# A segment-recurrent attention and gMLP kernel: a PSUM bank for the last V piece, another order of the V matmuls, and a new home for three side jobs

## The chip, the cores and the metric

The kernel runs on one core of one Trainium2 chip. The metric is the device time of a run in microseconds (us). Before the change nine runs have a median of 910.12 us, from 907.9 to 913.51.

Engine names in the profile: PE is TensorE (matrix multiply), PEld its weight load, ACT is ScalarE, DVE is VectorE, POOL is GpSimd, SP is SyncE, from whose queue (SPq) the transfers are issued.

## The reference

Two blocks run after each other on 2048 tokens of width 512. The first is attention with a recurrent memory: tokens come in 64 segments of 32, and the 8 memory rows that a segment uses are the first 8 output rows of the segment before. The second is a gated mixer over all tokens.

```python
for s in range(64):                        # recurrent: mem comes from the step before
    h = concat([mem, ln(x)[32*s:32*s+32]])  # 8 + 32 rows, 512 wide
    q, k, v = h @ Wq, h @ Wk, h @ Wv        # 32 heads of 128
    p = softmax(where(mask, q @ k.T * scale, -1e9))
    o = (p @ v) @ Wo
    mem = o[:8]; outs.append(o[8:])
h = x + concat(outs)
z = gelu(ln(h) @ w_in)
z1, z2 = z[:, :896], ln(z[:, 896:])
h2 = h + (z1 * (w_sp @ z2 + b_sp)) @ w_out
```

## The kernel before, in words

One function, `fast_path`, writes the program as a list of operations for each engine, in the order in which the Python code calls them. A helper class, `Emitter`, gives each operation the waits that its reads and writes need. A PSUM bank is one token `("ps", b)`: who writes a bank waits for all earlier readers of that bank. Each engine works through its list in order, so the order written by hand in the segment loop is the schedule.

The work has three stages: weights and first projections (to about 70 us of the trace), the segment loop (64 segments, to about 720 us), the mixer (the rest). The change lies in the segment loop.

Not all of a segment's 32 new rows need the chain of segments. In each segment only a 32-row piece of 8 memory rows and the first 24 x rows (`hT`) goes through the projections in the loop. The last 8 x rows of every segment are projected ahead, for 16 segments at a time: "X projections", in Q and K form (`qkx_mm`, L405, into `QTx`) and in V form (`vx_mm`, L424, through the DRAM buffer `vext_d` into `Vx`). The first 32 segments' X work is done before the loop; the rest is cut into 48 groups, in the list `gx`: 16 V groups for segments 0 to 15, then 32 Q/K groups for segments 16 to 47. Each loop step takes one group, in four PE parts and one eviction.

One segment `s` (with `j4 = s % 4`, `rb = s // 4`) runs as follows.

1. `QK` (L472): five pieces of Q and K matmuls, in 32-column tiles that run four at a time. After the first 8 matmuls stands `mem_out(s-1, 1)` (L648), which brings the second half of the new memory into `hT` (ACT, L656; the first half is copied by DVE, L654). Then come the operations that the previous segment left in the list `late`.
2. `QK_evac`: ACT copies each piece to `Tst` (L483), DVE transposes it to `QT` or `KT` (L491).
3. `S_half(s, 0)`: scores of heads 0 to 15 into bank 5 (L519, L525). ACT takes the exponent (`sm_exp`, L532). PE computes V of these heads (`V_half(s, 0)`, 16 matmuls of 512 columns, L573, bank 6), then the row sums (`sm_sums`, L539, L544). ACT takes the logarithm (`sm_ln`, L551) and the exponent of its negative (`sm_rcp`, L555); `sm_norm` multiplies on DVE (L559) and POOL (L563).
4. The same for heads 16 to 31, with V in two pieces: `V_half(s, 1)` into bank 2, evicted by DVE (L584), and into bank 7, evicted by ACT (L582). The second row sums stand in the middle of that last piece.
5. Two parts of the X group, then `PV_half(s, 0)` and `PV_half(s, 1)` (L592, L598; row tiles, four banks 0, 1, 6, 7, one per 32-row strip), then two more parts of the X group.
6. `cT_evac` (ACT L612, DVE L614): six evictions. `Wo` (L627): 56 and 8 matmuls, with `part_evac` (ACT, L639) and `mem_out(s, 0)` between.
7. Every fourth segment: `F_group` and `WoX_scatter` (L662, L687) gather the outputs of the previous four segments in bank 4, `F_add` (L667, DVE) adds x. `WoX_mm` (L677) is the Wo product of the X rows of four segments, a quarter (8 matmuls of 512 columns) at the end of each segment. `h_done` (L691 to L697) takes the statistics of the finished rows and stores them; `xn2_apply` and `xn2_store` (L700, L705) normalise and store them for the mixer.
8. x for two row blocks ahead: `load_x` at `j4 == 0`; at the end of `j4 == 1` `ln_inplace` (DVE statistics L353, L354, POOL power L355, L357, DVE apply L363); at the end of `j4 == 2` four PE transposes `xT` (L373), and in `late` an ACT copy from PSUM into `hT` (`ring_copy`, L383).

SP's queue in the loop: the load of `Vx` for two segments ahead (L446), x loads, stores of h and xn2, and one piece of the mixer's weight per odd segment (`wT_piece`, a transposing transfer L721 and a store L722). After segment 48 it also carries transposing transfers of xn2 (L714).

Of the kernel before, what the change touches and what calls it, by code (L numbers as in the profile page):

```python
# [169 lines left out]
def fast_path(nc, st, keep, A_x, A_mem0, A_Wq, A_Wk, A_Wv, A_Wo, A_seg_len, B_w_in, B_w_sp, B_b_sp, B_w_out, out):  # L170
    S = A_x.shape[1]
    D = A_x.shape[2]
# [80 lines left out]
    vext_d = nc.dram_tensor("vext_d", [NCK, 128, H * DH], BF, kind="Internal").ap()  # L253
    xn2_d = nc.dram_tensor("xn2_d", [RB, 128, D], BF, kind="Internal").ap()
    h_d = nc.dram_tensor("h_d", [RB, 128, D], BF, kind="Internal").ap()
    wT_d = nc.dram_tensor("wT_d", [S // 64, 128, RB, 64], BF, kind="Internal").ap()

    ps = st.enter_context(nc.psum_tensor("f_ps", [128, 8, 512], F32))
# [5 lines left out]
    def PB(b):  # L264
        return ("ps", b)
# [111 lines left out]
    def slot(s):  # L377
        return s % NSLOT

    def ring_copy(rb, bank):  # L380
        src = psb[:, bank, 0:512].rearrange("p (dc s c) -> p s dc c", dc=DC, s=4, c=SEG)[:, :, :, 0:XM]
        s0 = slot(4 * rb)
        act(lambda e: e.activation(out=hT[:, s0:s0 + 4, :, M:32], in_=src, func=ACT.Copy),  # L383
            reads=[PB(bank)], writes=[("hTx", rb % 3)])
# [14 lines left out]
    def qkx_mm(ck, i, bank, hhs=range(4)):  # L399
        mi, h0 = i // 8, 4 * (i % 8)  # L400
        ws = (w_q, w_k)[mi]
        for hh in hhs:
            h = h0 + hh
            for dc in range(DC):
                pe(lambda e, h=h, dc=dc, hh=hh: e.matmul(ps[:, bank, hh * 128:(hh + 1) * 128], lhsT=ws[:, dc, h * DH:(h + 1) * DH],  # L405
                                                         rhs=hTe[:, ck % 3, dc, :], start=(dc == 0), stop=(dc == DC - 1)),
                   reads=[("hTe", ck % 3), ("W", mi, h // 8)], writes=[PB(bank)])
# [44 lines left out]
    SB = 5  # L452
    UBK = (0, 1)
    PVB = (0, 1, 6, 7)
    VB = {(0, 0): 6, (1, 0): 2, (1, 1): 7}
    OB = 2
    XB = 3
    WXB = 4
# [95 lines left out]
    def sm_rcp(b):  # L554
        act(lambda e: e.activation(out=R_sb[:, b, :], in_=R_sb[:, b, :], func=ACT.Exp, scale=-1.0, bias=RBIAS),  # L555
            reads=[("R", b)], writes=[("R", b)])
# [113 lines left out]
    def load_h(rb):  # L670
        sp(lambda e: e.dma_start(hbuf[:, rb % 2, :], xr[:, rb, :]), writes=[("h", rb % 2)])

    def WoX_mm(rb, qr):
        for bg in range(8):
            b, g = bg // 4, bg % 4
            h = 16 * b + 4 * qr + g
            pe(lambda e, h=h, g=g, i=8 * qr + bg: e.matmul(ps[32 * g:32 * g + 32, WXB, :], lhsT=cTx[:, rb % 2, i, :], rhs=w_o[:, h, :],  # L677
                                                           start=(i < 4), stop=(i >= H - 4), tile_position=(0, 32 * g)),
               reads=[("cTx", rb % 2), ("Wo", h // 8)], writes=[PB(WXB)])
# [111 lines left out]
    gx = []  # L791

    def qkx_group(ck, i):
        gx.append([lambda hh=hh: qkx_mm(ck, i, XB, (hh,)) for hh in range(4)] + [lambda: qkx_evac(ck, i, XB, "dve")])

    def vx_group(ck, n):
        gx.append([lambda dc=dc: vx_mm(ck, n, XB, dc) for dc in range(DC)] + [lambda: vx_evac(ck, n, XB, "dve")])
# [21 lines left out]
               writes=[("wT", tb % 2, t)], after=after)  # L819

    lastop = {}
    qx_copy(0)
    for s in range(NSEG):
        j4 = s % 4
        rb = s // 4
        if j4 == 1 and rb > 0:
            load_h(rb - 1)
        if s == NSEG - 1:
            load_h(rb)
        if s % 2 == 1 and s // 2 < NWT:  # L830
            wT_piece(s // 2)
        if j4 == 0 and 2 <= rb + 2 < RB:
            load_x(rb + 2, 0)
        if s == 1:
            load_xe(3, 1)

        QK(s, QKP[0], (0, 1))
        if s > 0:
            mem_out(s - 1, 1)
            for f in late:  # L840
                f()
        QK(s, QKP[1], (0, 1))
        QK(s, QKP[0], (2, 3))
        QK_evac(QKP[0])
        QK(s, QKP[1], (2, 3))
        QK_evac(QKP[1])
        for piece in QKP[2:]:
            QK(s, piece)
            lastop["qk"[piece[3]]] = em.by_eng["pe"][-1]
            QK_evac(piece)  # L850
        if s == NSEG - 1:
            load_wT(0, [lastop["q"]])
        if s == 0:
            mask_pe()
        S_half(s, 0)
        sm_exp(0)
        V_half(s, 0)
        V_evac(0, "dve")
        sm_sums(0)
        sm_ln(0)  # L860
        S_half(s, 1)
        lastop["s"] = em.by_eng["pe"][-1]
        sm_exp(1)
        sm_rcp(0)
        if s == NSEG - 1:
            sp(lambda e: e.dma_start(w_in1, winr[:, :, 0:FH]), writes=["w_in1"], after=[lastop["s"], lastop["x"]])
            sp(lambda e: e.dma_start(bsp_b, bass.AP(B_b_sp.tensor, B_b_sp.offset, [[0, 128], [1, S]])), writes=["bsp"], after=[lastop["k"]])
            for r in range(8, RB - 2):
                xn2T_dma(r, [lastop["s"], lastop["x"]])
        V_half(s, 1, gs=(0, 2))  # L870
        V_evac(1, "dve", (0, 2))
        V_half(s, 1, (0, 1), gs=(2, 4))
        sm_sums(1)
        sm_ln(1)
        sm_rcp(1)
        V_half(s, 1, (2, 3), gs=(2, 4))
        lastop["v"] = em.by_eng["pe"][-1]
        V_evac(1, "act", (2, 4))
        sm_norm(0)
        sm_norm(1)  # L880
        if s + 1 < NSEG:
            qx_copy(s + 1)
            lastop["x"] = em.by_eng["pool"][-1]
# [29 lines left out]
        if j4 == 3 and rb > 0:  # L913
            late.append(lambda rb=rb: h_done(rb - 1))
        late += xs[4:]
        if j4 == 1 and 2 <= rb + 2 < RB:
            ln_inplace(0)
        if s == 3:
            ln_inplace(1)
# [3 lines left out]
        if s == 5:  # L923
            xT(1, FBK)
            late.append(lambda: xe_copy(3, FBK))
        if s + 1 < NSEG and s >= 3:
            WoX_mm((s + 1) // 4 - 1, (j4 + 1) % 4)
            if j4 == 2:
                late.append(lambda rb=rb: WoX_evac(rb - 1))
        if s + 1 == NSEG:  # L930
            for f in late:
                f()
        if s + 2 < NSEG:
            load_vx(s + 2)
        if j4 == 0 and rb >= 2:
            xn2_apply(rb - 2, rb % 2)
            xn2_store(rb - 2, rb % 2)
# [932 lines left out]
```

## Time and profile before

| | us |
|---|---|
| median of nine runs | 910.12 |
| the profiled execution, its own time | 914.51 |
| its span, first to last instruction | 912.8 |
| from the first to the last copy L654 (62 segments) | 649.0 |
| PE busy | 863.7 |
| PEld busy | 536.5 |
| DVE busy | 508.9 |
| ACT busy | 453.0 |
| POOL busy | 152.9 |

All lines of the profile come from one execution. A line of a timeline has the start in us, the busy time, the engine, the line of the code, the operation, out<-in with shapes, a count, and in brackets the engine's idle time before it with what ended it. A line of a table of stretches has start:end, length, then for PE, PEld, DVE, ACT and POOL the busy time with the number of instructions, then the granted PE clock, the share of the transfer engines, and GB/s. Matmuls overlap in the array, so the starts of PE's instructions tell more than their busy times.

### The profile page before, as it was taken

Reading aid. Unit: us, or ns where it says so; the run is one execution under the profiler, and the core shown is the slowest. Engines: PE = TensorE matmul, PEld = TensorE weight load, DVE = VectorE, ACT = ScalarE, POOL = GpSimd, SP = SyncE. Lnnn points to the kernel's source line nnn. Section 1 sums busy time; section 2 is a strip of 40 time slices with the busy share of each in tenths; the row PEclk is TensorE's granted clock in tenths of the full one; section 3 lists DMA queues with packets and bytes.
Section 4 is the critical chain, followed back from the end, with each engine's and each line's share of the span. In section 5 each row is a group of like instructions: output and inputs, shape, how many; then the busy total and the mean of one; then the engine's idle time right before and its main releaser. Section 6 shows DMA issues by size and latency. Waiting matters only on the chain.

```text
span 912.8 us, 48903 instructions
## 1 busy us (share of the span) xinstructions
PE 863.7 (95%) x22506; PEld 536.5 (59%) x22513; DVE 508.9 (56%) x1231; ACT 453.0 (50%) x1274; POOL 152.9 (17%) x403
## 2 busy tenths in 40 slices
PE   6989999999999999999999999889988999999998
PEld 6665566566666666666666666555555544444443
DVE  2435656565666666566656666555556554453433
ACT  2335566655565655666555656565666665400000
POOL 1401111121211211111212111121112122200000
PEclk9999999999999999999999999999999999999999
DMA  9971221322213020312112230514021392021201
GB/s 327 381 197 44 55 56 45 70 59 60 65 33 68 22 70 19 77 36 53 50 44 51 41 68 22 107 39 93 19 70 50 116 280 65 1 98 59 75 12 37
DMA packets 99587, 71.50 MB, mean 78 GB/s; under 512 B 62249, under 2 KB 84913, under 8 KB 99377
## 3 DMA queue, kind: packets, MB, share of 16 engines
q1 hardware_dynamic: 99376, 68.32, 27.5%
q8 instruction: 178, 2.92, 1.4%
q14 instruction: 33, 0.26, 0.1%
HBM read 39.46 MB, written 18.61 MB: 64 GB/s over the span
## 4 chain that ended last, share of the span: by engine, by line
PE 84%; ACT 8%; DVE 5%; issue 2%; POOL 1%; DMA 0%; SPq 0%; ACTq 0%
PE f_ps L472 21%; PE f_ps L627 14%; PE f_ps L573 11%; PE f_ps L1012 10%; PE f_ps L405 5%; PE f_ps L677 3%; PE f_ps L974 3%; PE f_ps L1005 3%; PE f_ps L592 3%; PE f_ps L1083 2%; PE f_ps L424 2%; ACT f_R_sb L555 2%; ACT f_R_sb L551 2%; ACT f_V_sb L582 2%; PE f_ps L539 1%
## 5 line engine op out<-in xcount | busy, mean ns | idle before, releaser
L472 PE MATMUL f_ps<-f_arena,f_hT 128*32 128x512 bf16 (+1 forms) x5120 | 240.3, 337 | 0.2
L472 PEld LDWEIGHTS f_ps<-f_arena,f_hT 128*32 128x32 bf16 x5120 | 125.5, 96 | 94.9 <-ACT f_hT L656 23.2
L483 ACT ACTIVATE f_Tst<-f_ps 128x512 bf16<-128x512 f32 (+1 forms) x320 | 148.8, 513 | 56.7 <-PE f_ps L472 46.8
L573 PE MATMUL f_ps<-f_arena,f_hT 128*32 128x256 bf16 (+1 forms) x3072 | 143.7, 308 | 0.8 <-issue 0.3
L627 PE MATMUL f_ps<-f_arena,f_cT 128*32 128x256 bf16 x4096 | 134.9, 277 | 7.0 <-ACT f_cT L612 5.0
L563 POOL TENSOR_TENSOR f_E_sb<-f_R_sb,f_E_sb 128x64 bf16<-128x64 f32 x128 | 44.2, 346 | 419.0 <-ACT f_R_sb L555 419.0
L627 PEld LDWEIGHTS f_ps<-f_arena,f_cT 128*32 128x32 bf16 x4096 | 95.1, 96 | 32.2 <-ACT f_cT L612 12.2
L491 DVE STREAM_TRANSPOSE f_QT<-f_Tst 128x256 uint32<-128x256 uint32 x128 | 56.9, 445 | 89.8 <-ACT f_Tst L483 89.8
L1012 PE MATMUL f_ps<-f_arena 128*128 128x512 bf16 x448 | 101.3, 379 | 2.4 <-DVE f_arena L1018 1.6
L639 ACT ACTIVATE f_part<-f_ps 128x256 bf16<-128x256 f32 x128 | 49.3, 385 | 93.3 <-PE f_ps L627 93.3
L614 DVE TENSOR_SCALAR f_cT<-f_ps 128x160 bf16<-128x160 f32 (+1 forms) x192 | 61.0, 374 | 43.3 <-PE f_ps L598 43.3
L584 DVE TENSOR_SCALAR f_V_sb<-f_ps 128x512 bf16<-128x512 f32 (+1 forms) x128 | 69.9, 559 | 17.1 <-PE f_ps L573 17.1
L573 PEld LDWEIGHTS f_ps<-f_arena,f_hT 128*32 128x32 bf16 x3072 | 66.6, 96 | 17.1 <-ACT f_Tst L483 1.8
L1012 PEld LDWEIGHTS f_ps<-f_arena 128*128 128x128 bf16 x448 | 43.5, 98 | 55.9 <-DVE f_arena L1018 2.6
L612 ACT ACTIVATE f_cT<-f_ps 128x160 bf16<-128x160 f32 (+1 forms) x192 | 53.0, 349 | 43.7 <-PE f_ps L598 43.7
L405 PE MATMUL f_ps<-f_hTe,f_arena 128*128 128x128 bf16 x1024 | 71.2, 224 | 0.7 <-ACT f_hTe L388 0.7
L491 DVE STREAM_TRANSPOSE f_KT<-f_Tst 128x128 uint32<-128x128 uint32 (+1 forms) x192 | 64.0, 339 | 3.6 <-ACT f_Tst L483 0.4
L405 PEld LDWEIGHTS f_ps<-f_hTe,f_arena 128*128 128x128 bf16 x1024 | 59.7, 100 | 10.1 <-issue 6.8
L592 PE MATMUL f_ps<-f_E_sb,f_V_sb 32*128 32x40 bf16 x2048 | 42.9, 178 | 19.4 <-ACT f_V_sb L582 14.7
L559 DVE TENSOR_TENSOR f_E_sb<-f_R_sb,f_E_sb 128x160 bf16<-128x160 f32 x128 | 48.6, 380 | 19.9 <-ACT f_R_sb L555 19.9
L551 ACT ACTIVATE f_R_sb<-f_ps 128x160 f32<-128x160 f32 x128 | 39.0, 305 | 40.3 <-PE f_ps L544 40.3
L654 DVE CAST f_hT<-f_ps 128x16 bf16<-128x16 f32 x63 | 11.0, 175 | 78.3 <-PE f_ps L648 78.3
(103 smaller groups left out, 1073.9 us busy)
## 6 DMA issues: line engine op xcount, KB each, us to landing
wT_d<-f_wst SPq DMA_DIRECT2D x32, 256.0 KB, 2.8
f_arena<-wT_d SPq DMA_DIRECT2D x32, 256.0 KB, 4.3
f_arena<-in_A_Wq_dram SPq DMA_DIRECT2D x4, 1024.0 KB, 9.2
f_arena<-in_A_Wv_dram SPq DMA_DIRECT2D x4, 1024.0 KB, 13.1
f_arena<-in_A_Wk_dram SPq DMA_DIRECT2D x4, 1024.0 KB, 14.5
f_arena<-in_A_Wo_dram SPq DMA_DIRECT2D x4, 1024.0 KB, 9.4
f_Vx<-vext_d SPq DMA_DIRECT2D x64, 64.0 KB, 2.7
f_xn<-in_A_x_dram SPq DMA_DIRECT2D x17, 128.0 KB, 2.6
```

Source lines behind the costliest of these rows:

```text
L405: pe(lambda e, h=h, dc=dc, hh=hh: e.matmul(ps[:, bank, hh * 128:(hh + 1) * 128], lhsT=ws[:, dc, h * DH:(h + 1) * DH], rhs=hTe[:, ck % 3, d ...
L472: pe(lambda e, dc=dc, c=c, rhs=rhs: e.matmul(ps[32 * c:32 * c + 32, bank, 0:32 * nh], lhsT=hT[:, sl, dc, :], rhs=rhs, start=(dc == 0), sto ...
L483: act(lambda e: e.activation(out=st_.rearrange("p (hp i r) -> p hp i r", i=32, r=2), in_=ps[:, bank, 0:64 * np_].rearrange("p (hp r i) -> ...
L491: dve(lambda e: e.transpose(out=dst, in_=src), reads=tok, writes=[(nm, b, k) for k in halves(b, p0, np_)])
L551: act(lambda e: e.activation(out=R_sb[:, b, :], in_=ps[:, bank, 224:384], func=ACT.Ln, scale=LNS), reads=[PB(bank)], writes=[("R", b)])
L573: pe(lambda e, dc=dc, c=c, c0=c0: e.matmul(ps[32 * c:32 * c + 32, bank, 0:w], lhsT=hT[:, sl, dc, :], rhs=w_v[:, dc, c0:c0 + w], start=(dc ...
L584: dve(lambda e: e.tensor_scalar(out=dst, in0=src, scalar1=VSC, scalar2=None, op0=ALU.mult), reads=[PB(bank)], writes=tok)
L592: pe(lambda e, q=q, c=c, g=g, c0=c0: e.matmul(ps[:, PVB[c], c0:c0 + 40], lhsT=V_sb[q, b, g * 128:(g + 1) * 128], rhs=E_sb[q, b, g * 40:(g ...
L612: act(lambda e: e.activation(out=dst, in_=src, func=ACT.Copy, scale=UNSC), reads=[PB(PVB[c])], writes=tok)
L614: dve(lambda e: e.tensor_scalar(out=dst, in0=src, scalar1=UNSC, scalar2=None, op0=ALU.mult), reads=[PB(PVB[c])], writes=tok)
L627: pe(lambda e, h=h, g=g, i=i, b=b, c=c: e.matmul(ps[32 * g:32 * g + 32, bank, 0:d1 - d0], lhsT=cTh[:, i, 8:40], rhs=w_o[:, h, d0:d1], star ...
L1012: pe(lambda e: e.matmul(ps[:, bank, 0:TB], lhsT=z2[:, sc, fb * 128:(fb + 1) * 128], rhs=wTb[tb % 2][:, :, sc, :], start=(sc == 0), stop=(s ...
```

## The change

The edits are all in the segment loop and its helpers.

- **Banks.** V of heads 16 to 31: the first piece goes to bank 7, the last to bank 2.
- **V order.** Three quarters of `V_half(s, 0)` stand before the first row sums, the last quarter after `S_half(s, 1)`. The last V piece stands whole after the second row sums. `sm_norm(0)` comes ahead of the eviction of the first piece of `V_half(s, 1)`.
- **X projections.** Q and K groups use the new `qkx_cols`: 64 matmuls per group in four 32-column tiles, in place of 16 matmuls 128 wide. The eviction of a group follows the cT evictions at once (at `j4 == 3` it stays in `late`). At `j4 == 2` the first part of the next group is drawn ahead to the end of the segment.
- **WoX.** The 32 matmuls of a block are cut into 8 steps of four, in the list `wq`: one step ahead of `PV_half` at `j4` 0 to 2, two at the end of `j4` 0 and 1, one at the end of `j4` 3. From segment 48 on: three steps ahead of `PV_half`, none at the end.
- **F_group and WoX_scatter** stand ahead of `PV_half`.
- **x.** Statistics run a segment before the apply, both in `late`. In place of `xT` and `ring_copy`, `x_flip` stores the normalised rows to the DRAM buffer `xs_d` and reads them back with a transposing transfer; `ring_fill` copies them to `hT` on DVE. `xn2_apply` and `xn2_store` move from the end of `j4 == 0` to `late` of `j4 == 1`.

```diff
+    xs_d = nc.dram_tensor("xs_d", [RB + 1, 128, D], BF, kind="Internal").ap()
+    def x_flip(j, i, dst, tok):
+        t, rd = xbuf(j)
+        sp(lambda e: e.dma_start(xs_d[i], t), reads=rd, writes=[("xs", i)])
+        sp(lambda e: e.dma_start_transpose(out=dst, in_=xs_d[i]), reads=[("xs", i)], writes=[tok])
+
+    def ring_fill(rb):
+        src = xn[:, 1, :].rearrange("p (dc s c) -> p s dc c", dc=DC, s=4, c=SEG)[:, :, :, 0:XM]
+        s0 = slot(4 * rb)
+        dve(lambda e: e.tensor_copy(out=hT[:, s0:s0 + 4, :, M:32], in_=src), reads=[("xn", 1)], writes=[("hTx", rb % 3)])
...
+    def qkx_cols(ck, i, bank, hh):
+        mi, h = i // 8, 4 * (i % 8) + hh
+        ws = (w_q, w_k)[mi]
+        for dc in range(DC):
+            for c in range(4):
+                pe(lambda e, dc=dc, c=c: e.matmul(ps[32 * c:32 * c + 32, bank, hh * 128:(hh + 1) * 128],
+                                                  lhsT=ws[:, dc, h * DH + 32 * c:h * DH + 32 * c + 32], rhs=hTe[:, ck % 3, dc, :],
+                                                  start=(dc == 0), stop=(dc == DC - 1), tile_position=(0, 32 * c)),
                    reads=[("hTe", ck % 3), ("W", mi, h // 8)], writes=[PB(bank)])
...
-    VB = {(0, 0): 6, (1, 0): 2, (1, 1): 7}
+    VB = {(0, 0): 6, (1, 0): 7, (1, 1): 2}
...
-    def WoX_mm(rb, qr):
-        for bg in range(8):
+    def WoX_mm(rb, qr, bgs=range(8)):
+        for bg in bgs:
...
-        V_half(s, 0)
-        V_evac(0, "dve")
+        V_half(s, 0, (0, 1, 2))
         sm_sums(0)
         sm_ln(0)
         S_half(s, 1)
         lastop["s"] = em.by_eng["pe"][-1]
         sm_exp(1)
         sm_rcp(0)
+        V_half(s, 0, (3,))
+        V_evac(0, "dve")
...
         V_half(s, 1, gs=(0, 2))
+        sm_norm(0)
         V_evac(1, "dve", (0, 2))
-        V_half(s, 1, (0, 1), gs=(2, 4))
         sm_sums(1)
         sm_ln(1)
         sm_rcp(1)
-        V_half(s, 1, (2, 3), gs=(2, 4))
+        V_half(s, 1, gs=(2, 4))
         lastop["v"] = em.by_eng["pe"][-1]
         V_evac(1, "act", (2, 4))
-        sm_norm(0)
         sm_norm(1)
...
-        xs = gx.pop(0) if gx else []
         late = []
-        for f in xs[:2]:
-            f()
-        PV_half(s, 0)
-        PV_half(s, 1)
-        for f in xs[2:4]:
-            f()
+        nw1, nw4 = ((1, 1, 1, 0)[j4], (2, 2, 0, 1)[j4]) if s < 3 * CK else (3, 0)
         if j4 == 3 and rb > 0:
             F_group(rb - 1, WXB)
             WoX_scatter(rb - 1, WXB)
+        xs = gx.pop(0) if gx else []
+        fill = xs[:4]
+        if j4 == 3 and s < 3 * CK:
+            fill = xs[1:4]
+        for f in fill[:-2]:
+            f()
+        for f in wq[:nw1]:
+            f()
+        del wq[:nw1]
+        PV_half(s, 0)
+        PV_half(s, 1)
+        for f in fill[-2:]:
+            f()
...
         if j4 == 3 and rb > 0:
             F_add(rb - 1, WXB)
+            late += xs[4:]
+            late.append(lambda rb=rb: h_done(rb - 1))
+        else:
+            for f in xs[4:]:
+                f()
...
-        late += xs[4:]
-        if j4 == 1 and 2 <= rb + 2 < RB:
-            ln_inplace(0)
-        if j4 == 2 and 2 <= rb + 2 < RB:
-            xT(0, FBK)
-            late.append(lambda rb=rb: ring_copy(rb + 2, FBK))
-        if s + 1 < NSEG and s >= 3:
-            WoX_mm((s + 1) // 4 - 1, (j4 + 1) % 4)
+        if j4 == 0 and 2 <= rb + 2 < RB:
+            late.append(lambda: ln_stats(0))
+        if j4 == 0 and 2 <= rb + 1 < RB:
+            late.append(lambda rb=rb: ring_fill(rb + 1))
+        if j4 == 1 and 2 <= rb + 2 < RB:
+            late.append(lambda rb=rb: (ln_apply(0), x_flip(0, rb, xn[:, 1, :].rearrange("p (dc c) -> p dc c", dc=DC), ("xn", 1))))
+        if j4 == 1 and rb >= 2:
+            late.append(lambda rb=rb: (xn2_apply(rb - 2, rb % 2), xn2_store(rb - 2, rb % 2)))
+        if s + 1 < NSEG:
+            if j4 == 3:
+                wq.extend(lambda rb=rb, k=k: WoX_mm(rb, k // 2, range(4 * (k % 2), 4 * (k % 2) + 4)) for k in range(8))
+            elif j4 == 2 and gx:
+                gx[0][0]()
+            for f in wq[:nw4]:
+                f()
+            del wq[:nw4]
```

More of the change, by code (lines that the diff above doesn't have):

```diff
@@ L406, in qkx_mm @@
                                                          rhs=hTe[:, ck % 3, dc, :], start=(dc == 0), stop=(dc == DC - 1)),
+                   reads=[("hTe", ck % 3), ("W", mi, h // 8)], writes=[PB(bank)])
+    def qkx_cols(ck, i, bank, hh):
[6 more added lines that the diff above has]
+                                                  start=(dc == 0), stop=(dc == DC - 1), tile_position=(0, 32 * c)),
                    reads=[("hTe", ck % 3), ("W", mi, h // 8)], writes=[PB(bank)])
@@ L793, in qkx_group @@
     def qkx_group(ck, i):
-        gx.append([lambda hh=hh: qkx_mm(ck, i, XB, (hh,)) for hh in range(4)] + [lambda: qkx_evac(ck, i, XB, "dve")])
+        gx.append([lambda hh=hh: qkx_cols(ck, i, XB, hh) for hh in range(4)] + [lambda: qkx_evac(ck, i, XB, "dve")])
     def vx_group(ck, n):
@@ L821, in fast_path @@
     lastop = {}
+    wq = []
     qx_copy(0)
@@ L834, in fast_path @@
         if s == 1:
-            load_xe(3, 1)
+            load_xe(3, 7)
         QK(s, QKP[0], (0, 1))
@@ L912, in fast_path @@
         part_evac(s, OB2, OC, D)
-        if j4 == 3 and rb > 0:
-            late.append(lambda rb=rb: h_done(rb - 1))
-        late += xs[4:]
+        if j4 == 0 and 2 <= rb + 2 < RB:
+            late.append(lambda: ln_stats(0))
+        if j4 == 0 and 2 <= rb + 1 < RB:
+            late.append(lambda rb=rb: ring_fill(rb + 1))
         if j4 == 1 and 2 <= rb + 2 < RB:
-            ln_inplace(0)
+            late.append(lambda rb=rb: (ln_apply(0), x_flip(0, rb, xn[:, 1, :].rearrange("p (dc c) -> p dc c", dc=DC), ("xn", 1))))
+        if s == 2:
+            late.append(lambda: ln_stats(7))
         if s == 3:
-            ln_inplace(1)
-        if j4 == 2 and 2 <= rb + 2 < RB:
-            xT(0, FBK)
-            late.append(lambda rb=rb: ring_copy(rb + 2, FBK))
-        if s == 5:
-            xT(1, FBK)
-            late.append(lambda: xe_copy(3, FBK))
-        if s + 1 < NSEG and s >= 3:
-            WoX_mm((s + 1) // 4 - 1, (j4 + 1) % 4)
-            if j4 == 2:
-                late.append(lambda rb=rb: WoX_evac(rb - 1))
-        if s + 1 == NSEG:
+            late.append(lambda: (ln_apply(7), x_flip(7, RB, hTe[:, 0, :, :], ("hTe", 0))))
+        if j4 == 1 and rb >= 2:
+            late.append(lambda rb=rb: (xn2_apply(rb - 2, rb % 2), xn2_store(rb - 2, rb % 2)))
+        if j4 == 2 and rb > 0:
+            assert not wq
+            late.append(lambda rb=rb: WoX_evac(rb - 1))
+        if s + 1 < NSEG:
[6 more added lines that the diff above has]
+            del wq[:nw4]
+        else:
             for f in late:
@@ L934, in fast_path @@
             load_vx(s + 2)
-        if j4 == 0 and rb >= 2:
-            xn2_apply(rb - 2, rb % 2)
-            xn2_store(rb - 2, rb % 2)
         if s == 3 * CK:
```

## The prediction, made before the changed kernel was run

> **What bounds the kernel now.** I read the page's engine table and chain shares first, then cut the segment loop into stretches, then followed one segment instruction by instruction.
>
> ```profile
> PE 863.7 (95%) x22506; PEld 536.5 (59%) x22513; DVE 508.9 (56%) x1231; ACT 453.0 (50%) x1274; POOL 152.9 (17%) x403
> PE 84%; ACT 8%; DVE 5%; issue 2%; POOL 1%; DMA 0%; SPq 0%; ACTq 0%
> ```
>
> TensorE (PE) looks like the bound. The next view says otherwise. It gives busy time per stretch, cut at the starts of the memory copy L654 (once per segment): four consecutive segments with X projections, then one late segment without.
>
> ```profile
> 395.26:405.36 10.10, 9.94 (x338) 6.68 (x329) 6.62 (x17) 6.06 (x18) 2.35 (x6) 1.00 0.08 22
> 405.36:415.51 10.15, 9.99 (x339) 6.70 (x330) 6.18 (x17) 6.07 (x18) 1.56 (x4) 1.00 0.41 96
> 415.51:426.13 10.62, 10.32 (x336) 6.57 (x324) 6.76 (x19) 5.96 (x18) 2.35 (x6) 1.00 0.38 58
> 426.13:437.09 10.96, 10.80 (x351) 7.36 (x346) 6.56 (x17) 6.83 (x20) 1.56 (x4) 1.00 0.06 17
> 689.37:699.46 10.09, 9.03 (x322) 5.88 (x314) 6.04 (x17) 6.07 (x18) 2.35 (x6) 1.00 0.08 24
> ```
>
> The last stretch has no X projection on PE (9.03 us busy, not 9.94) and is as long: 10.09 against 10.10 us. So the base segment is a latency chain across engines, and PE work in it is filler. Taking work off PE gains nothing there by itself. The third and fourth stretches are 0.52 and 0.86 us longer: something is added to the chain in them.
>
> The timeline of the attention-value step in one segment:
>
> ```profile
> 411.96 0.34 ACT L555 ACTIVATE f_R_sb<-f_R_sb 128x160 f32<-128x160 f32 x1
> 412.20 0.37 ACT L582 ACTIVATE f_V_sb<-f_ps 128x256 bf16<-128x256 f32 x1
> 412.33 0.32 DVE L559 TENSOR_TENSOR f_E_sb<-f_R_sb,f_E_sb 128x160 bf16<-128x160 f32 x1 [0.31 <-ACT f_R_sb L555]
> 412.44 0.38 POOL L563 TENSOR_TENSOR f_E_sb<-f_R_sb,f_E_sb 128x64 bf16<-128x64 f32 x1 [0.59 <-ACT f_R_sb L555]
> ...
> 412.62 0.26 PE L592 MATMUL f_ps<-f_E_sb,f_V_sb 32*128 32x40 bf16 x13 [0.16 <-ACT f_V_sb L582]
> ...
> 412.86 0.28 PE L592 MATMUL f_ps<-f_E_sb,f_V_sb 32*128 32x40 bf16 x16
> ```
>
> PV_half(0) starts at 412.27, stops after three matmuls and waits for the ScalarE eviction of the last V piece, because its fourth matmul writes bank 7, which that eviction reads. So PV_half(1) starts at 412.86, though its normalised input was ready at 412.65.
>
> The long stretches, and the hand-over to the next segment:
>
> ```profile
> 415.73 0.39 ACT L639 ACTIVATE f_part<-f_ps 128x256 bf16<-128x256 f32 x1 [0.56 <-PE f_ps L627]
> 416.16 0.31 PEld L648 LDWEIGHTS f_ps<-f_G_sb,f_part 128*32 128x32 bf16 x8
> 416.36 0.20 PE L648 MATMUL f_ps<-f_G_sb,f_part 128*32 128x8 bf16 x8
> ...
> 418.03 0.41 DVE L363 TENSOR_SCALAR f_xn<-f_xn,f_mv,f_rs 128x512 bf16<-128x512 bf16 x1 [1.00 <-POOL f_rs L357]
> ...
> 419.77 0.17 PEld L519 LDWEIGHTS f_ps<-f_QT,f_KT 128*32 128x32 bf16 x16 [0.38 <-DVE f_KT L491]
> ...
> 426.22 0.40 PE L373 MATMUL f_ps<-f_ident,f_xn 128*128 128x128 bf16 x4
> ```
>
> VectorE stands 1.00 us in the x LayerNorm waiting for POOL's power, with the X eviction and the Q/K transposes queued behind; PE then misses the K transposes at 419.77. And the memory matmul could begin at 416.16, but PE is still in its fill until 416.36.
>
> [...] eight V matmuls before a 128-wide X group hold PE 0.33 us (411.39 to 411.72), before a column-tiled X group 0.22 (97.45 to 97.67). [...] The trace's full-width X matmuls are slower: eight in 0.55 us, 69 ns each; its column-tiled 40-column scores agree (16 on four tiles in 0.10 us, so 25 ns per tile). [...] here the same form (L714) holds SP's queue 1.28 us and lands after 3.6.
>
> **The change part by part**, in the time of the profiled execution (914.5 us; span 912.8; it lies 4.4 above the median 910.1).
>
> *x LayerNorm and transpose.* Removed: 15 PE transposes of x (0.33 us each, plus 0.10 us of mode switch by the start times, 0.43) and the PSUM copies on ScalarE (0.49). They stand after the last Wo matmuls and push everything behind them: 15 x 0.43 = 6.5. Splitting statistics and apply over two segments ends the 1.00 us VectorE wait; PE lost about 0.5 per segment to it, in some 12 segments: 6.0. Added on VectorE: a 128x384 copy, not in the trace; nearest are the 128x512 apply (0.41) and, as an upper end, the PSUM evictions (0.69). I take 0.4. With bn_stats 0.69 and bn_aggr 0.18 that is 1.3 us between the mask copy's end (416.2) and the first Q transpose, which comes at about 418.0 in a segment without stall: hidden, 0.5 us spare. In the following segment apply plus the moved xn2 apply take 0.8 in the same gap. Added on SP: a store (1.7 us to landing like h_d), a wait for that landing, and a transpose (1.3 to issue, 3.6 to land), once in four segments. Behind them stand the xn2 store and the Vx load for two segments later, some 20 us ahead of need; the transposed x is used three segments later. Zero; only a queue blocked for over 10 us would show. **Gain 12.**
>
> *F and scatter matmuls* move from after PV to before it, into a wait: they cost 0.43 in 11 segments (the rest of the fourth stretch's 0.86). One X quarter, 0.21, leaves that place. **Gain 4.6.**
>
> *V order and bank.* V_half(0) before the first sums is cut from 16 matmuls to 12, so PE idles there, but the sums start when exp allows: 410.26, not 410.35. Score half 1, exp and second sums follow: 411.28 becomes 411.20; reciprocal ends 412.22, not 412.30. VectorE: the V(0) eviction starts later, 410.95 for 410.58, since its last four matmuls follow score half 1. Then by start spacings 0.67 (V), about 0.3 (normalise, now ahead), 0.34 (V): second normalise at 412.27, end 412.6, against 412.65 before. Bank 7 is now free after the VectorE eviction, about 412.3. PE: sums 0.11, V 0.43, X half group 0.43, four WoX 0.21, mode switch 0.11: at PV by 412.49. PV_half(0) needs 0.19, so PV_half(1) starts near 412.68 instead of 412.86. Ends of this estimate: 0, if VectorE or PE comes later than reckoned, and 0.20, the whole wait. I take 0.15 x 63 segments. **Gain 9.5.** What is late next is PE itself, level with VectorE and POOL.
>
> *Less fill after Wo.* Before, 0.43 of WoX plus 0.43 of QK stood between the last Wo and the memory matmul. In two segments of four (24 before segment 48), and in all 15 from 48 on, 0.21 or none of WoX remains. The eviction path allows 0.19 earlier (416.16 plus its load, against 416.36). Ends 0 and 0.19; I take 0.15 x 39. **Gain 5.9.**
>
> *Column-tiled X projections.* 32 groups of 64 matmuls in place of 16: 64 x 128 columns over four tiles, 0.85 us if weights hide, for 1.10. The trace does not show 128-column column tiles. Upper end: each tile alternates a 96 ns load and 53 ns of columns, 16 x 149 ns = 2.4 us. The scores, where each tile does load and matmul within 25 ns, exclude most of that; I take 0.85. After PV the saved time is lost to the cT evictions (PE already waits there on L612), before PV it is inside the reckoning above. Gain of its own: 0. Moving the X eviction to just after the cT evictions takes VectorE 0.68 us in a gap of 1.25. Zero; were the gap gone, the memory copy L654 would be late.
>
> Sum: 12 + 4.6 + 9.5 + 5.9 = 32. 914.5 - 32 = 882.5 for such an execution; on the median, 910.1 - 32 = 878.
>
> **Rivals.** (1) *The chain does not shorten:* VectorE's later V(0) eviction, or the fuller fill before PV, makes the second half as late as the bank did, and the hand-over gains nothing. For: three engines meet within 0.1 us. Against: VectorE idled 0.31 before that normalise. Then only 12 + 4.6 = 17 remain: 893. (2) *Both chain terms come in whole,* 63 x 0.20 + 39 x 0.19 = 20, plus 17, and outlying segments (one has 0.6 us more in PV) give 2 more: 910 - 39 = 871. (3) *Slower: weight loads of the column tiles do not hide.* Place: the X halves around PV in segments 16 to 47. At 2.4 us a group costs 1.55 more than 0.85; some 0.2 fits into the cT wait, so 1.35 x 32 = 43, against 32 gained: 921. It decides from 32/32 + 0.2 + 0.85, about 2.05 us per group. The scores speak against it.
>
> **How the numbers follow.** Likeliest case 0.60 (own range 873 to 886), rival 1 0.21, rival 2 0.13, rival 3 0.04, no net change by something unseen 0.02. The range 867 to 895 reaches over rivals 1 and 2. A measurement of this kernel tells about 0.3% from no change. Faster 0.94, same 0.02, slower 0.04.
>
> **What would show it.** Segments without extras at about 9.95 us or less, those with little WoX behind Wo near 9.8; no stretch of 10.6 or 10.9; no wait of PV on the V eviction, but on a normalise; no VectorE wait on POOL in the x LayerNorm; X groups of 64 matmuls in about 0.85. The prediction is wrong if PV starts as late as now, if the column tiles run above 1.1 us, or if VectorE's transposes wait for the ring copy.

## The result, and the profile after

The changed kernel is slower: 932.26 us, median of 10 runs (929.35 to 936.46), against 910.66 before (31 runs). The ratio is 1.0243, with a 95% interval of 1.0225 to 1.0262. The forecast was 878 us, with a range from 867 to 895. The profiled execution after took 933.18 us with a span of 931.3 (before: 914.51 and 912.8). Medians below leave out two executions of one run, e3, that lay over 1.5% above its fastest.

Where did the 18.5 us of span come from? I added up the 62 intervals between the starts of the memory copy (L675 after, L654 before), one per segment, by what X work a segment carries:

```
                         before          after        difference
V X, segments 1-15       157.1 (10.47)   152.1 (10.14)    -5.0
Q/K X, segments 16-47    335.7 (10.49)   368.2 (11.51)   +32.5
no X, segments 48-62     156.2 (10.41)   151.3 (10.09)    -4.8
before the first copy     70.7            65.9            -4.8
after the last copy      193.1           193.8            +0.7
sum in us (mean of one segment)
```

So everywhere else the loop became faster, and the segments with the column-tiled projections lost 1.02 us each. Here is the table of stretches of the kernel after: four stretches of that kind, then one without X work.

```profile
265.31:277.28 11.97, 10.27 (x385) 6.54 (x376) 7.09 (x18) 6.06 (x18) 2.42 (x6) 1.00 0.32 68
367.22:378.83 11.61, 10.41 (x389) 7.26 (x383) 6.65 (x18) 6.06 (x18) 2.41 (x6) 1.00 0.02 5
378.83:390.42 11.59, 10.51 (x390) 6.96 (x383) 6.37 (x17) 6.07 (x18) 1.62 (x4) 1.00 0.43 93
390.42:401.99 11.57, 10.08 (x386) 6.86 (x376) 5.73 (x16) 6.55 (x19) 1.63 (x4) 1.00 0.07 17
708.26:718.02 9.76, 9.32 (x324) 5.69 (x316) 5.91 (x16) 6.06 (x18) 2.41 (x6) 1.00 0.49 99
```

The last stretch is what I forecast for a segment with little fill (near 9.8). In the others PE is busy for 10.1 to 10.5 us and the stretch lasts 11.6 to 12.0: PE stands idle for over a microsecond, and does so with a transfer share of 0.02 as with 0.43. What is new in the columns is the count: 385 to 390 matmuls and 376 to 383 loads, where before had 336 to 351 and 324 to 346.

What does PE wait for? The view of waits of the kernel after (engine, what, line, releaser: us in total, times, longest):

```profile
PEld f_ps L648 <- issue: 27.4, 22, 2.4
PE f_ps L648 <- issue: 22.6, 22, 2.3
...
PE f_ps L425 <- issue: 6.6, 8, 1.4
```

For nothing that the profile shows. "Issue" is what the profile calls a wait for which it shows no releaser. The matmul lines of all stages together wait about 48 us on it, against 6 us in the kernel before, of which one wait ahead of the loop takes 3.1. In the page's chain after, "issue" now holds 6% where it held 2%; these are the engine table, the instruction queue, the chain's shares and the two groups concerned:

```profile
PE 858.1 (92%) x23982; PEld 529.4 (57%) x23989; DVE 504.5 (54%) x1245; ACT 450.3 (48%) x1259; POOL 157.1 (17%) x403
...
q8 instruction: 190, 3.11, 1.4%
...
PE 91%; issue 6%; DVE 2%; ACT 1%; DMA 0%; POOL 0%; SPq 0%
...
L648 PE MATMUL f_ps<-f_arena,f_cT 128*32 128x256 bf16 x4096 | 139.6, 275 | 28.9 <-issue 22.6
...
L425 PE MATMUL f_ps<-f_hTe,f_arena 128*32 128x128 bf16 x2048 | 43.5, 220 | 6.8 <-issue 6.6
```

And the same three rows of the page before:

```profile
q8 instruction: 178, 2.92, 1.4%
...
L627 PE MATMUL f_ps<-f_arena,f_cT 128*32 128x256 bf16 x4096 | 134.9, 277 | 7.0 <-ACT f_cT L612 5.0
...
L405 PE MATMUL f_ps<-f_hTe,f_arena 128*128 128x128 bf16 x1024 | 71.2, 224 | 0.7 <-ACT f_hTe L388 0.7
```

PE has 1476 more matmuls (48 x 32 from the column tiles, less 60 transposes) and as many more weight loads, 2952 instructions. The instruction queue has 12 more packets, each of 16384 bytes in the trace. 2952 / 12 = 246, so one packet holds some 250 instructions. With 256 the count fits all thirteen traces: PE's matmuls and loads, from 44899 to 48091, divided by 256 give the number of packets, from 178 to 190, less 2.1 to 2.6. So I read these packets as PE's program; the trace names their queue "instruction" and no more.

One stall, in PE's timeline of the kernel after:

```profile
248.75 0.63 PE L425 MATMUL f_ps<-f_hTe,f_arena 128*32 128x128 bf16 x32
249.30 0.62 PE L648 MATMUL f_ps<-f_arena,f_cT 128*32 128x256 bf16 x16
252.08 1.17 PE L648 MATMUL f_ps<-f_arena,f_cT 128*32 128x256 bf16 x36 [2.17 <-issue]
```

The Wo group stops after 16 of its matmuls, though the profile shows nothing that it waits for, and goes on 2.17 us later. The packets of the instruction queue around it, from the trace:

```
start us   249.49  253.97  257.71  261.89  265.88  269.77  273.92  277.40   (16384 bytes each)
PE resumes 252.08 (packet ended 250.58), 260.30 (258.89), 264.07 (262.82), 272.18 (270.73), 276.24 (274.88)
```

Each of these stalls ends 1.25 to 1.50 us after the end of a packet, and stalls lie 127, 128, 256 or 383 matmuls apart: with a load to each matmul that is one, two or three packets. The whole stretch says the same. In segments 16 to 47 there are 44 gaps of over 0.4 us between the starts of two PE instructions, 50 us in sum. All 44 wait on "issue" and end 1.19 to 1.60 us after a packet, and from one to the next PE starts one, two or three times 256 instructions, less two at most. They stand in ten different lines of the code: what counts is the place in the packet, not the work that stands there.

A packet takes about 1 us (0.88 to 1.18 here) and one comes every 3.8 to 3.9 us (medians of the three thirds of the loop; 3.99 in this stretch). 256 / 3.85 is 66 instructions per us. This rate alone would prove nothing, since the packets follow PE's progress: in the mixer of the same trace, where PE starts fewer instructions, five intervals in a row last 25 to 31 us, with 232 to 274 PE instructions in each. It is the stalls that show PE waiting for its program. A Q/K X segment has about 758 PE instructions after (662 on average before, and 96 more): 758 / 66 = 11.5 us, the time measured, and 662 / 66 = 10.0, just under the 10.49 of before.

### The profile page after: what moved, and what is told of

It is laid out like the page before. It is cut to its first block, busy times and chain, and to the rows that moved or that the text cites. A ratio compares the mean times of both kernels' runs of the same rounds, so it can differ in the third digit from the quotient of the medians.

```text
span 931.3 us, 51906 instructions
## 1 busy us (share of the span) xinstructions
PE 858.1 (92%) x23982; PEld 529.4 (57%) x23989; DVE 504.5 (54%) x1245; ACT 450.3 (48%) x1259; POOL 157.1 (17%) x403
## 4 chain that ended last, share of the span: by engine, by line
PE 91%; issue 6%; DVE 2%; ACT 1%; DMA 0%; POOL 0%; SPq 0%
PE f_ps L493 25%; PE f_ps L648 13%; PE f_ps L594 12%; PE f_ps L1049 10%; PE f_ps L425 4%; PE f_ps L698 3%; PE f_ps L416 3%; PE f_ps L445 3%; PE f_ps L1011 3%; PE f_ps L1042 3%; PE f_ps L613 2%; PE f_ps L1120 2%; PE f_ps L560 2%; PE f_ps L540 1%; PE f_ps L619 1%
## 5 line engine op out<-in xcount | busy, mean ns | idle before, releaser
L493 PE MATMUL f_ps<-f_arena,f_hT 128*32 128x512 bf16 (+1 forms) x5120 | 243.1, 337 | 4.0 <-issue 2.9
L493 PEld LDWEIGHTS f_ps<-f_arena,f_hT 128*32 128x32 bf16 x5120 | 124.7, 96 | 98.3 <-ACT f_hT L677 22.6
L648 PE MATMUL f_ps<-f_arena,f_cT 128*32 128x256 bf16 x4096 | 139.6, 275 | 28.9 <-issue 22.6
L648 PEld LDWEIGHTS f_ps<-f_arena,f_cT 128*32 128x32 bf16 x4096 | 96.9, 95 | 53.4 <-issue 27.4
L584 POOL TENSOR_TENSOR f_E_sb<-f_R_sb,f_E_sb 128x64 bf16<-128x64 f32 x128 | 48.2, 377 | 409.0 <-ACT f_R_sb L576 409.0
L605 DVE TENSOR_SCALAR f_V_sb<-f_ps 128x512 bf16<-128x512 f32 (+1 forms) x128 | 70.6, 552 | 41.3 <-PE f_ps L594 41.3
L594 PEld LDWEIGHTS f_ps<-f_arena,f_hT 128*32 128x32 bf16 x3072 | 69.4, 96 | 16.1 <-issue 3.4
L675 DVE CAST f_hT<-f_ps 128x16 bf16<-128x16 f32 x63 | 11.0, 175 | 82.0 <-PE f_ps L669 82.0
L1055 DVE TENSOR_TENSOR f_arena<-f_ps,f_arena 128x512 f32<-128x512 f32 x28 | 19.3, 691 | 57.8 <-PE f_ps L1049 57.8
L425 PE MATMUL f_ps<-f_hTe,f_arena 128*32 128x128 bf16 x2048 | 43.5, 220 | 6.8 <-issue 6.6
L580 DVE TENSOR_TENSOR f_E_sb<-f_R_sb,f_E_sb 128x160 bf16<-128x160 f32 x128 | 45.6, 356 | 1.0 <-ACT f_R_sb L576 1.0
L698 PE MATMUL f_ps<-f_arena,f_cTx 128*32 128x512 bf16 x512 | 44.1, 382 | 1.2 <-issue 1.2
```

Of the source, the lines that this page charges most:

```text
L425: pe(lambda e, dc=dc, c=c: e.matmul(ps[32 * c:32 * c + 32, bank, hh * 128:(hh + 1) * 128], lhsT=ws[:, dc, h * DH + 32 * c:h * DH + 32 * c ...
L493: pe(lambda e, dc=dc, c=c, rhs=rhs: e.matmul(ps[32 * c:32 * c + 32, bank, 0:32 * nh], lhsT=hT[:, sl, dc, :], rhs=rhs, start=(dc == 0), sto ...
L594: pe(lambda e, dc=dc, c=c, c0=c0: e.matmul(ps[32 * c:32 * c + 32, bank, 0:w], lhsT=hT[:, sl, dc, :], rhs=w_v[:, dc, c0:c0 + w], start=(dc ...
L605: dve(lambda e: e.tensor_scalar(out=dst, in0=src, scalar1=VSC, scalar2=None, op0=ALU.mult), reads=[PB(bank)], writes=tok)
L648: pe(lambda e, h=h, g=g, i=i, b=b, c=c: e.matmul(ps[32 * g:32 * g + 32, bank, 0:d1 - d0], lhsT=cTh[:, i, 8:40], rhs=w_o[:, h, d0:d1], star ...
```

## The experiments

My theory: PE's program arrives at some 66 instructions per us; the column tiles add 96 instructions to a segment, and the segment becomes as long as its program takes to arrive. Rivals: the column-tiled groups themselves are slow on the array (weight loads, changes of mode); the weight pieces' transfers, which fall into these segments, hold up the packets; or one of the moved parts costs.

**e1_wide_x**, the kernel after with the wide X matmuls of before:

```
-        gx.append([lambda hh=hh: qkx_cols(ck, i, XB, hh) for hh in range(4)] + ...
+        gx.append([lambda hh=hh: qkx_mm(ck, i, XB, (hh,)) for hh in range(4)] + ...
```

> The changed kernel with one part undone: the Q/K X groups are again 16 matmuls 128 wide instead of 64 in column tiles; order, banks, WoX steps and x transfers stay changed. Theory (PE's instruction stream): in segments 16 to 47 of the changed kernel PE gets about 66 instructions per us, 758 per segment, 11.5 us. With 662 per segment the same rate gives 10.05 us, so 32 x 1.46 = 47 less than 932: about 885. Rival (the new order of V or the x transfers through DRAM make the X segments long): they stay, 925 to 932. Rival (column tiles of 128 columns are slow in the array, by weight loads): also about 885, but then the tiles are slow wherever they stand.

Measured: 891.18 us, 0.9796 of before (0.9754 to 0.9837), where after is 1.0243. One line is worth 41 us: the other parts together are a gain of 2%. Its stretches, three with Q/K X work and one without:

```profile
349.80:359.96 10.16, 10.16 (x339) 6.84 (x330) 6.64 (x18) 6.05 (x18) 2.41 (x6) 1.00 0.02 6
359.96:370.27 10.31, 10.31 (x340) 6.62 (x328) 6.37 (x17) 6.05 (x18) 1.62 (x4) 1.00 0.29 73
370.27:380.35 10.08, 10.08 (x339) 6.61 (x332) 5.73 (x16) 6.54 (x19) 1.62 (x4) 1.00 0.17 50
654.72:664.48 9.76, 9.31 (x320) 5.77 (x312) 5.72 (x16) 6.54 (x19) 1.61 (x4) 1.00 0.02 4
```

With X work PE is busy from end to end (10.16 of 10.16), so these stretches show no wait that could still be shortened. In segments 16 to 47 one gap of over 0.4 us is left where the kernel after has 44.

**e2_before_cols**, the kernel before with the column tiles and nothing else of the change (the edit of e1, the other way round, and `qkx_cols` added):

> The kernel before with one part of the change alone: its Q/K X groups in column tiles (64 matmuls per group). Theory (instruction stream): 760 PE instructions per segment at 66 per us make 11.5 us in place of 10.5 in 32 segments, so 910 + 33 = about 943, with idle time of PE that nothing but issue explains, in steps of about 128 matmuls. Rival (order and x transfers): about 910. Rival (weight loads do not hide in column tiles): slower too, but the time lies in the X groups themselves, over 1.1 us per group.

Measured: 935.72 us, 1.0271 (1.0213 to 1.0328); Q/K X segments 11.23 us where before has 10.49 (11.5 expected), the others hardly changed (157.2 and 154.2 in sum). So the loss comes with that part alone. The waits on "issue" are there as well; L414 is its X group, L637 its Wo group:

```profile
PE f_ps L637 <- issue: 8.6, 14, 1.2
PE f_ps L414 <- issue: 6.0, 10, 0.9
```

**e3_small_mm**, e1 with 48 matmuls of 8 columns more, behind the attention-value step of every segment from 48 on, where there is no X work. They write to a bank that nobody reads there:

```
+        if s >= 3 * CK:
+            for k in range(48):
+                c = k % 4
+                pe(lambda e, c=c: e.matmul(ps[32*c:32*c+32, XB, 0:M], lhsT=ident[:, 32*c:32*c+32], rhs=G_sb[:, :],
+                                           start=True, stop=True, tile_position=(0, 32 * c)), ...
```

> The first kernel of this call plus 48 matmuls of 8 columns into an unused bank in each of the last 16 segments, which have no X work; they stand behind PV, where PE waits about 0.6 us for the cT evictions, and need about 0.3 us. Their results are not used. Theory (instruction stream): 720 instead of 624 PE instructions per segment, at 66 per us 10.9 in place of 9.77 us: 16 x 1.15 = 18 more than the first kernel of this call, about 903. Rival (array time or weight loads of the X tiles): the 0.3 us hide, no more than 2 us in all.

Measured: 907.0 us, 0.9969 (0.9943 to 0.9994), 15.8 us over e1 (13.2 in the profiled intervals 48 to 62). The segments without X go from 9.77 to 10.91 us by median; those with X stay (10.20). Two of the changed stretches, and what PE waits for (L928 are the added matmuls, L648 is Wo):

```profile
641.15:652.15 11.00, 9.97 (x372) 6.63 (x364) 5.30 (x16) 6.05 (x18) 1.62 (x4) 1.00 0.02 5
652.15:663.06 10.91, 9.79 (x368) 6.41 (x360) 5.45 (x16) 6.05 (x18) 1.62 (x4) 1.00 0.38 77
...
PE f_ps L648 <- issue: 7.3, 12, 1.7
PE f_ps L928 <- issue: 3.7, 4, 1.7
```

PE is busy for only 0.5 to 0.7 us more than in e1's 9.31, but the segment is 1.14 longer and PE idles for a full microsecond of it. There is no X projection here, no 128-column tile and no projection weight, only the number of instructions is that of the column tiles: (372 + 364) / 11.00 = 67 per us, (368 + 360) / 10.91 = 67. This is the experiment that separates the count from the work. The rate is not a fixed one, though: two of the loaded segments took 9.77 us, as without the load, with 723 instructions, 74 per us.

**e4_two_tiles**, `qkx_cols` with two tiles of 64 columns, so 32 matmuls a segment instead of 64 (wide: 16):

```
-            for c in range(4):
-                pe(... ps[32 * c:32 * c + 32, ...], lhsT=ws[:, dc, h * DH + 32 * c:h * DH + 32 * c + 32], ... tile_position=(0, 32 * c))
+            for c in range(2):
+                pe(... ps[64 * c:64 * c + 64, ...], lhsT=ws[:, dc, h * DH + 64 * c:h * DH + 64 * c + 64], ... tile_position=(0, 64 * c))
```

> The changed kernel with the Q/K X groups in two tiles of 64 columns: 32 matmuls per group. Theory (instruction stream): 694 PE instructions per segment, at 66 per us 10.5 us, so 32 x 0.48 = 15 above the first kernel of this call: about 900, between 885 and 932 as the instruction count is. Rival (the mode of 32-column tiles is slow): no linear step; about as the first kernel if only 32-wide tiles are slow.

Measured: 899.45 us, 0.9899 (0.986 to 0.9937), Q/K X segments 10.49. By the count, (662 + 32) / 66 = 10.5. One size between the two gives the time between.

**w1_after_quiet**, the kernel after with the weight pieces taken out of segments 16 to 47, so that no such transfer falls into the X segments:

```
-        if s % 2 == 1 and s // 2 < NWT:
-            wT_piece(s // 2)
+        if s < 16:
+            wT_piece(s)
+        if s >= 48:
+            wT_piece(s - 32)
```

> The changed kernel (932 us) with the 32 pieces of the mixer's weight (256 KB in, 256 KB out each) moved out of segments 16 to 47 into the first and last 16, where the PE stream is thinner. If the fetch of PE's instructions has a rate of its own, about 66 per us whatever else is moved: segments 16 to 47 stay at 11.4 to 11.5 us, 930 to 935 in all. If it is slowed by the kernel's own transfers: these segments fall towards 10.3, the total by up to 30.

Measured: 930.68 us, 1.0236 (1.019 to 1.0281); X segments 11.18 for 11.51. So these transfers account for 0.3 us of a segment, some 10 us in all, of which 3.6 come back before the first copy (69.5 for 65.9). 758 / 11.18 = 68 per us is reached without them.

Four runs took back one of the moved parts each, from e1:

**d1_pe_transpose**: LayerNorm in place, transposes of x on PE and the PSUM copies, as before.

```
-            late.append(lambda rb=rb: (ln_apply(0), x_flip(0, rb, ...)))
+            ln_inplace(0)
+        if j4 == 2 and 2 <= rb + 2 < RB:
+            xT(0, FBK)
+            late.append(lambda rb=rb: ring_copy(rb + 2, FBK))
```

> The kernel with wide X groups (891 us) with the x path as before: LayerNorm of x in one piece on VectorE at the end of every fourth segment, four PE transposes a segment later, ScalarE copy. Forecast term of the prediction: 12 us, so about 903. If the x path is free either way: 891.

**d2_f_after_pv**: `F_group` and `WoX_scatter` behind the attention-value step.

```
-        if j4 == 3 and rb > 0:
-            F_group(rb - 1, WXB)
-            WoX_scatter(rb - 1, WXB)
         ... the attention-value step and the rest of the fill ...
+        if j4 == 3 and rb > 0:
+            F_group(rb - 1, WXB)
+            WoX_scatter(rb - 1, WXB)
```

> The kernel with wide X groups (891 us) with the F and scatter matmuls behind PV again. Forecast term of the prediction: 0.43 us in 11 segments, 4.6, so about 895 to 896; nothing from segment 48 on, where the cT wait hides them. If PE is the bound of these segments now, the place doesn't matter: 891.

**d3_v_order_bank** (V order, bank and place of the normalise as before) and **d3b_bank_only** (the bank alone):

```
-    VB = {(0, 0): 6, (1, 0): 7, (1, 1): 2}
+    VB = {(0, 0): 6, (1, 0): 2, (1, 1): 7}
```

> The kernel with wide X groups (891 us) with the V order, the place of the first normalise and the banks as before. Forecast term of the prediction: 0.15 us in each of 63 segments, 9.5, so about 900; segments without X work at 9.92 in place of 9.77. Rival: the gain came from less fill alone, then 891 and 9.77.

> The kernel with wide X groups (891 us), V order changed, but the banks of the two last V pieces as before, so that PV's fourth matmul again waits for the ScalarE eviction of the last V piece. If the bank is what the V term rests on: the whole of it is lost, about 900, segments without X work near 9.92. If the order is what counts: 891.

```
            us       ratio (95%)               Q/K X    no X (typical)    what the part is worth by the trace
e1          891.18   0.9796 (0.9754-0.9837)    10.20    9.77
d1          895.63   0.9823 (0.9779-0.9867)    10.40    9.76              0.8 per four segments with Q/K X
d2          896.73   0.9827 (0.9788-0.9867)    10.30    9.77              0.33 in every fourth with Q/K X
d3          895.79   0.9829 (0.9792-0.9867)    10.18    9.91              0.15 per segment without X, 0 with
d3b         893.78   0.9797 (0.9757-0.9836)    10.21    9.84              0.07 per segment without X, 0 with
```

The four ran beside a before of 913.28 us, e1 beside one of 909.39, so the ratios are to be compared. They differ from e1's by 0.0001 to 0.0033, inside the intervals: on the clock alone none of the parts is told from nothing, and the 903 forecast for d1 and the 900 for d3 and d3b did not come. The traces point to small gains, but one trace each: over all 62 intervals d1 is 8.2 us longer than e1, d2 7.6, d3 4.4 and d3b 6.2, though d3b takes back less than d3. Single segments scatter by up to 2 us (segment 48: 12.25 in e1, 14.35 in d3b).

Two last runs looked for a faster order. **e5_swap** is e1 with the WoX step ahead of the X half group:

```
-        for f in fill[:-2]:
-            f()
         for f in wq[:nw1]:
             f()
+        for f in fill[:-2]:
+            f()
```

> The kernel with wide X groups (891 us) with the four WoX matmuls ahead of the X half group instead of behind it, so that the array changes its tiling mode once less ahead of PV (V and WoX in column tiles, then the wide X, then PV): 0.1 us in 24 segments, 2.6, so about 888 or 0.977 of the kernel before. If the fetch is the bound of these segments: no change, 0.980.

**e6_swap_quiet** is e5 with the weight pieces moved as in w1:

> The kernel of the run before this one in the call (WoX ahead of the wide X half group) with the weight pieces out of segments 16 to 47 as well. Rate of its own: within 2 us of the run before. Slowed by transfers: up to 5 us less, since these segments, at 10.2 us, stand 0.4 above those without X work, and part of that is array time.

Measured: 893.11 us, 0.9797 (0.9771 to 0.9823), and 897.27, 0.9854 (0.9818 to 0.9889). X segments are 10.13 and 10.09 for e1's 10.20, which is nothing in the total. That e6 is slower than e5 in the profiled executions (a span of 894.4 for 890.1) lies before the first copy, 69.4 us for 65.0, as it does in w1, the other kernel that puts a weight piece into each of the first 16 segments. No version is told from e1 as faster; e1 lies 2% under before.

## Why the prediction was wrong, point by point

**The failed step is "Column-tiled X projections ... Gain of its own: 0".** (The title of this document leaves out this part of the change, which decided the result.) The prediction priced the 64 matmuls in time on the array, bounded that time from both sides, and was right about it. PE's timeline of the kernel after, two half groups of 32 and what follows each:

```profile
386.58 0.62 PE L425 MATMUL f_ps<-f_hTe,f_arena 128*32 128x128 bf16 x32
387.03 0.39 PE L698 MATMUL f_ps<-f_arena,f_cTx 128*32 128x512 bf16 x4
...
388.03 0.63 PE L425 MATMUL f_ps<-f_hTe,f_arena 128*32 128x128 bf16 x32
388.50 1.80 PE L648 MATMUL f_ps<-f_arena,f_cT 128*32 128x256 bf16 x56
```

0.45 and 0.47 us by the starts, 0.92 for a group against 0.85 forecast. Four column tiles start within 11 ns of each other, and the next four 56 ns after them, though the trace shows each of their weight loads at 97 ns (L425, median of 2048): here the tiles do load and multiply in parallel. The forecast's 0.85 was an estimate, and the trace of before bears it out; these are its lines for a full-width X half group and for eight WoX matmuls on four tiles, with what follows each:

```profile
411.72 0.62 PE L405 MATMUL f_ps<-f_hTe,f_arena 128*128 128x128 bf16 x8
412.27 0.20 PE L592 MATMUL f_ps<-f_E_sb,f_V_sb 32*128 32x40 bf16 x3
...
415.50 0.60 PE L677 MATMUL f_ps<-f_arena,f_cTx 128*32 128x512 bf16 x8
415.93 0.60 PE L472 MATMUL f_ps<-f_arena,f_hT 128*32 128x512 bf16 x8
```

Two WoX matmuls on each tile, 1024 columns, take 0.43 us by the starts (busy times, 377 ns for one, overlap), so 128 columns take 53 to 54 ns and the 2048 columns of a group's tile 0.86 us. One reading behind the price was wrong. The prediction took 69 ns for a full-width X matmul, from 0.55 us to the next instruction; in the same trace the eight start 56 ns apart (411.72 to 412.12, the first step 66), and the next instruction, in row tiles (32*128 in the line above), starts 0.15 us after the last of them, 0.10 more than that step. The prediction's 0.33 and 0.22 us, before a full-width and before a column-tiled group, differ by 0.11 as well. So the array does the same work in the same time either way (8 x 56 = 0.45 us for a full-width half group, 0.45 for the 32 tiles), and the tiles save at most these 0.10 to 0.11 us at a change of mode. The 25 ns of the scores hold tile by tile too: over the four tiles they start every 6 ns (16 in 0.10 us).

What the prediction did not count are the instructions. 16 matmuls with 16 loads became 64 with 64, 96 more per segment; at 66 per us that is 1.45 us, in 32 segments 47 us. Measured, after against e1: 368.2 - 326.5 = 41.7 us in these segments, and 41 in the medians. (The 47 is more because e1's segments last 10.20 and not the 10.03 of their program; their stretches show PE busy all the time.)

Could the page have told it? In part. Before had 662 instructions in 10.49 us in such a segment, 63 per us, and its chain already gave 2% to "issue", a wait that I read past. The limit itself hardly showed there: these segments have two gaps of over 0.4 us on "issue", and other waits came first. But the question of what else grows fourfold belonged into the working, and the stream of the program was a resource without a price: it should have been bounded like the others, with the 63 per us that the trace shows as the only safe value. 758 / 63 = 12.0 us for a segment would have been the upper end, slower than before.

**Rival 3** had the sign and the place, the X halves in segments 16 to 47, by the wrong mechanism, and it carried the whole chance of 0.04 that was given to a slower kernel. Its weight loads hide, with 0.92 us for a group. The stalls mostly stand in the Wo group that follows (22.6 us at L648, 6.6 at L425), which the rival would not explain.

**V order and bank** (0.15 x 63 forecast): the mechanism came in. A segment without X in the kernel after, around the attention-value step (L613):

```profile
714.84 0.36 ACT L603 ACTIVATE f_V_sb<-f_ps 128x256 bf16<-128x256 f32 x1
714.97 0.33 DVE L580 TENSOR_TENSOR f_E_sb<-f_R_sb,f_E_sb 128x160 bf16<-128x160 f32 x1
...
715.22 0.27 PE L613 MATMUL f_ps<-f_E_sb,f_V_sb 32*128 32x40 bf16 x16
...
715.37 0.28 PE L613 MATMUL f_ps<-f_E_sb,f_V_sb 32*128 32x40 bf16 x16
```

The first half runs through its 16 matmuls, and the second starts 0.15 us after it, where before the second half came 0.59 after the start of the first. The wait itself moved rather than ended: PE's weight loads for this step wait 46 times, 16.3 us in all, for VectorE's V eviction (L605), where the prediction wanted no wait on a V eviction at all. The size is 0.15 per segment by d3, of which the bank alone gives 0.07, but only where there is no X work: with it, 10.18 stands against 10.20. The step "x 63" failed; in 32 segments PE has no slack, and what the chain gives back is filled by PE's own work.

**x LayerNorm and transpose** (12): 8.2 us by the sums of d1's segments and 4.8 by its span, neither told from nothing on the clock. In segments with Q/K X it is 0.8 per four segments, near the 0.43 for PE and 0.5 for the wait that were forecast. The wait of VectorE on POOL is gone (0.8 us in all, 15.8 before), the ring copy takes 0.229 us for the 0.4 taken, and nothing queues behind the store (1.7 us to landing) and the transpose (3.3).

**F and scatter** (0.43): 0.33 in every fourth segment with Q/K X, somewhat under the forecast.

**Less fill after Wo** (0.15 x 39): not tried alone. Segments of little fill are at 9.76, as forecast.

**The rest of the miss.** Without the column tiles the forecast would still have been 13 us too low (891 for 878). In the profiled executions e1 is 23.6 under before, not 32: the terms put about 17 us of gain into the Q/K X segments (V 4.8, fill 2.4, F 3.4, x 6.4), and e1 shows 9.2; its stretches there leave PE no idle time. Of the 23.6, 4.6 are luck: they lie before the first copy (66.1 us for 70.7), where no term stands, and no run here settles where they come from. Some 5 us more is the profiled execution of before, which lay 4.4 over its median; the medians of e1 and of the runs beside it differ by 18.2. The first step, "PE work in it is filler", was true of before and ceased to be true in these segments once 0.3 us was taken from the chain (10.49 to 10.20).

## What to carry to other kernels

Count the instructions of a change as well as the time of its work: an edit that splits each matmul in four needs four times the program, and in the Q/K X segments of the kernel after PE started 66 instructions (33 matmuls with their loads) per us. As an estimate from these 33, a long run of matmuls that take less than about 30 ns each with their loads is paid at that rate; the 74 per us of single segments in e3 show that it is no fixed one. When a stage on an engine gets denser, work out its instructions per us before and after. And a gain on a latency chain ends where the filler fills it: price each term separately for stages with slack and stages without.

## What the runs showed of the hardware

- The packets that I read as PE's program have 16384 bytes and, by the counts of thirteen traces, about 256 PE instructions (190 packets for 47971 instructions in the kernel after). The eight around the stall shown above took 0.88 to 1.18 us each. In the loop of the kernel after one came every 3.8 to 3.9 us; in its slower mixer every 25 to 31 us, with 232 to 274 PE instructions between. PE stood on "issue" for up to 2.4 us. The 44 longer stalls in segments 16 to 47 of the kernel after ended 1.19 to 1.60 us after a packet, one, two or three times 256 instructions apart, less two at most. Why the next packet comes so late, when it takes 1 us itself, stays open.
- The rates reached over the Q/K X segments: 65 PE instructions per us in e1, 66 in after, 67.5 in e2, 68 in w1; 67 in e3's two stretches above, and 74 in single segments.
- Four column tiles of 32 take 14 to 15 ns per 128-column matmul with a fresh load (32 in 0.45 to 0.47 us), 136 to 142 instructions per us in such a run, twice the 66 of the whole segment. Full-width ones start 56 ns apart, so eight of them and 32 tiles take the array the same 0.45 us. Eight full-width ones hold PE 0.55 us up to an instruction in another mode.
